# A new order of work, with the weights' casts on ScalarE and GpSimd, in attention followed by mixture of depths

## The chip, the cores and the metric

The kernel runs on one core of a Trainium2 chip. The core has TensorE (PE) for matrix products, VectorE (DVE), ScalarE (ACT) and GpSimd (POOL) for the rest, and SyncE (SP), which here only issues transfers. Each engine takes its instructions strictly in the order in which they were written, and waits for other engines or for transfers by semaphores. The metric is the time of one execution on the device in microseconds.

## The reference

The inputs are q, k and v of shape (8, 8, 576, 64): batch, heads, positions, head size. Attention is causal over a window of 128 positions, with a bias that falls with the distance at a slope of its own for each head. Its output, put together over the heads, is x of shape (8, 576, 512). Then each batch picks the 128 positions with the largest gate score and runs them through two matrices of weights:

```
scores = where(0 <= i - j < 128, q k^T / 8 - slope_h * (i - j), -1e9)
x      = softmax(scores) v                  (heads side by side: 512 columns)
s      = x . w_gate                         (one score a position)
top    = the 128 positions of largest s, for each batch
out    = x, and for positions in top:
out    = x + sigmoid(s) * (relu(x w1) w2)   (w1: 512x1024, w2: 1024x512)
```

All inputs and the output are 32-bit floats in main memory.

## The kernel before

The kernel works batch by batch. Within a batch, heads are taken in four pairs (c = 0 to 3), and the positions in five tiles of 128 (the last one half full). The steps of one batch b are small functions, and each has a one-letter name:

- Loads: `L` brings q or k, `l` brings v. All are issued by SyncE in the order before. Casts to bf16: `Q` for q and k (lines 315 to 323), `C` for v (lines 388 to 397). The cast helper `_cast` (line 304) uses ACT.copy on ScalarE, an affine_select with a condition that always holds on GpSimd (line 307), and tensor_copy on VectorE (line 313).
- `T`: transposes of q and k on TensorE (line 331) into one of two PSUM buffers named `mx`; `V`: the copy out of PSUM into qT or kT (lines 337 and 339), which frees that buffer.
- `S`: scores of one head pair, the bias and mask as products first (line 414), q times k after (line 430), into one PSUM buffer `sc`. `X`: one exponential of 128x2048 on ScalarE (line 439). `A`: product with v, which has a column of ones for the sum (lines 454 and 457), into one PSUM buffer `at`. `N`: division by the sum into x (lines 464 and 466, VectorE).
- `P`: the store of x to `out` (lines 477 and 481). `G`, `g` and `J`: gate scores (line 506, VectorE). `B`, `H`, `b`, `h`: the scores spread along a row. `M`: comparisons (line 547, VectorE), `R`, `r`: the rank of each position. `O`: a one-hot matrix of the picked positions (line 589 on GpSimd or 593 on VectorE). `K`, `k`: the list of picked positions.
- `D`: the picked rows of x as a product with the one-hot matrix (line 623), `v` the copy out; `W`, `w`: product with w1 (line 637) and relu (lines 647 and 649); `Z`, `z`: product with w2 (line 654), scaled by the gate (lines 661 and 664); `F`: GpSimd adds the result into the picked rows of `out` by an indirect transfer (line 667). Every `F` waits until the transfer of the `F` before it has landed.

The weights are loaded in eight chunks of 512 KB, `U0` to `U3` for w1 and `U4` to `U7` for w2 (lines 682 and 685), and cast by `d0` to `d7` (`cast_w`, line 690). A word d without an engine goes to VectorE at line 698. The chunks have no buffer of their own: they use two halves of `x_buf[2]`, one for even and one for odd chunks, so that a load waits for the cast of the chunk two before it. `x_buf[2]` then holds x of batches 4 and 7, so `N40` waits for the last weight cast.

Nothing decides the order at run time. The string ORDER (line 731) lists all 729 steps as words: the letter, the batch, the numbers of the step, and after a slash the engine (A, D, P, S) where there is a choice. The last lines of the kernel walk through it, so the order of the words is the order of each engine's queue, and the order in which buffers are handed on. `S13`, for example, is the scores of batch 1, pair 3; `C021/D` casts tile 2, half 1 of batch 0's v on VectorE; `V00t/D` copies the tail of batch 0's transposed q out of PSUM on VectorE.

The line that names the engine of a weight cast:

```
(load_w(int(name[1])) if f == "U" else cast_w(int(name[1]), e))
```

Of the kernel before, what the change touches and what calls it, by code (L numbers as in the profile page):

```python
# [26 lines left out]
def kernel(  # L27
# [376 lines left out]
    P, sc_t = {}, {}  # L404
# [274 lines left out]
    def load_w(i):  # L679
        t = wst[i] = w_flat[:, 1024 * (i % 2):1024 * (i % 2) + 1024]  # L680
        if i < 4:
            SP.dma_start(out=t, in_=moe_w1[128 * i:128 * (i + 1), :])
        else:
            i -= 4
            SP.dma_start(
                out=t.rearrange("p (c f) -> p c f", c=2),
                in_=moe_w2[256 * i:256 * (i + 1), :].rearrange(
                    "(c p) f -> p c f", p=128))
# [39 lines left out]
    def gate_spread(eng):  # L728
        _copy(eng, wg_bc.rearrange("p (i x) -> p i x", i=NDC), wg_t.pop("r"))

    ORDER = """
        c3 L011/S c0 L010/S L00t/S L001/S L000/S L01t/S l01 c1 L002/S
        qL l02 L003/S c2 L012/S l00 Q011/A L013/S L10 L11 l12 c6 T011
        Q010/D c8 Q00t/A c5 c7 T010 V011/A Q000/A Q01t/D V010/A T000
        c92 c4 Q001/A T00t V000/A C021/D T01t c90 V01t/A V00t/D Q002/A
        C031/D T001 S00 C041/D V001/A C020/P qT T002 X00 C030/P qe
        Q003/D Q012/D L20 l10 c91 C040/P T012 V002/A V012/D T003 S01
        C011/P C010/D qB X01 C000/D C001/D V003/D A00 Q013/D N00 T013
        L21 l11 S02 Q1000/P Q1011/A V013/D A01 Q1010/A Q1001/P qb/D
        X02 L30 N01 T102 T100 V102/D Q11t/P Q1111/A A02 c93 Q1110/P  # L740
        V100/A T112 N02 S03 C140/P V112/A T101 Q1100/P X03 V101/D
        Q1101/P T110 L31 V110/D T111 l22 Q2001/P l21 C141/A A03
        Q2011/P V111/A N03 l20 Q2010/P T202 Q2000/A S10 C111/P V202/D
        P00 P01 l32 C100/A C101/P T200 X10 T201 G02 G04 G00 Q21t/A S11
        G01 Q2100/A C110/A Q2110/P V200/D l30 V201/D T210 C120/P
        C121/A X11 C130/P L40 V210/D T212 C131/P A10 l31 G03 S12
        Q2111/P V212/D Q3011/A N10 Q3001/P H0 B0 X12 Q2101/P h0/D A11
        b0/D Q3010/P L41 T211 U1 M01 Q3000/P V211/A S13 M02 Q3110/P
        L50 U0 N11 X13 Q3100/P Q31t/P M03 A12 M00 C241/P T310 C231/A
        S20 N12 Q3101/P V310/A C221/P T301 M04 A13 C220/P V301/D  # L750
        C230/A R0 C201/P Q3111/A r0 T302 N13 C210/P T312 X20 C200/P
        V302/D P11 P10 C240/P G11 l42 E0 S21 V312/A L51 G10 C211/A X21
        G14 A20 T311 G13 T300 G12 V311/A S22 C340/P N20 O0/P V300/A H1
        A21 h1/D e0 X22 B1 N21 b1/D Q4000/A S23 M14 C301/P M12 E1 K0
# [16 lines left out]
        D2 X50 C510/P M34 k1 A43 C501/P M32 T610 v2/D C521/P C531/A
        S51 C511/P N43 V610/A W11 C530/P l70 X51 M30 C520/P T611 G42
        F0 l71 A50 G41 w11/A S52 P40 P41 G40 V611/A T601 G43 V601/A
        G44 B4 W20 N50 b4/A C640/P X52 Q7001/P H4 w20/D A51 Q7010/P
        h4/D T602 N51 R3 Q7000/P V602/A S53 Q7011/P r3 M40 C620/A T612
        C621/P A52 X53 V612/D T702 C600/P e3 Z1 O3/D C611/P N52 E4
        V702/A S60 C641/P z1/A M44 C631/P M41 A53 X60 Q7100/P M43 K2
        D3 k2 C610/P M42 C601/P N53 W21 v3/A C630/P Q71t/A W30 P50 G53
        F1 w21/A T700 G50 w30/A S61 G51 V700/A R4 G52 X61 T712 A60 r4
        Q7110/P V712/D T701 N60 Q7101/P B5 b5/A S62 G54 V701/A A61  # L780
        O4/D X62 H5 T710 Q7111/P h5/D e4 Z2 C740/P M54 N61 C720/P
        V710/A C710/P M52 S63 z2/A M53 C731/P M51 K3 A62 X63 C741/P k3
        T711 C721/P N62 D4 C730/P V711/A M50 C700/P A63 C711/P v4/A
        N63 S70 C701/P R5 X70 P60 G61 P51 P61 K4 r5 k4 W41 G60 E5 G63
        S71 w41/A G62 W31 X71 G64 A70 O5/P w31/D B6 N70 H6 S72 b6/A
# [107 lines left out]
```

The softmax here doesn't subtract the row's maximum and nothing guards it: scores larger than these inputs give would overflow.

## Time and profile before

| | before |
|---|---|
| time, median of 3 runs | 177.33 us (175.79 to 177.97) |
| span of the profiled execution | 175.2 us |
| TensorE busy | 130.3 us (74%) |
| VectorE busy | 133.5 us (76%) |
| ScalarE busy | 121.0 us (69%) |
| GpSimd busy | 105.1 us (60%) |
| moved by transfers | 44.38 MB, mean 253 GB/s |
| first exponential starts | 14.65 us |
| last exponential (X73) starts | 142.10 us |

A share of the span is an average over stages. The kernel has a start, in which the first loads, casts and transposes follow each other; a long middle, in which attention of one batch runs beside the transposes of the next and the second part of an earlier one; and a tail after the last exponential, in which only the picked positions are left. A line of a timeline gives the start, the duration, the engine, the line of the kernel, the operation with its tiles, and in brackets how long the engine had been idle before it and what ended that.

### The profile page before, as it was taken

Reading aid. Unit: us, or ns where it says so; the run is one execution under the profiler, and the core shown is the slowest. Engines: PE = TensorE matmul, PEld = TensorE weight load, DVE = VectorE, ACT = ScalarE, POOL = GpSimd, SP = SyncE. Lnnn points to the kernel's source line nnn. Section 1 sums busy time; section 2 is a strip of 40 time slices with the busy share of each in tenths; the row PEclk is TensorE's granted clock in tenths of the full one; section 3 lists DMA queues with packets and bytes.
Section 4 is the critical chain, followed back from the end, with each engine's and each line's share of the span. In section 5 each row is a group of like instructions: output and inputs, shape, how many; then the busy total and the mean of one; then the engine's idle time right before and its main releaser. Section 6 shows DMA issues by size and latency. Waiting matters only on the chain. (4 is left out here: it accounts for less than half of the span.)

```text
span 175.2 us, 5068 instructions
## 1 busy us (share of the span) xinstructions
PE 130.3 (74%) x2023; PEld 102.8 (59%) x2029; DVE 133.5 (76%) x383; ACT 121.0 (69%) x143; POOL 105.1 (60%) x171
## 2 busy tenths in 40 slices
PE   0426988667787866888974998999998999989100
PEld 0214766456665764576753787698697767686000
DVE  6655896999897899999955997999899997833000
ACT  4626497989979978449956899999887874532100
POOL 3761377599899917983318994988199903123330
PEclk9999999999969999699978999999999999999855
DMA  4899999999999995937999999999908044644224
GB/s 143 250 300 372 349 348 358 388 314 338 307 365 392 406 377 190 344 90 244 337 326 327 278 350 262 362 370 360 320 26 290 14 60 175 160 60 63 19 42 60
DMA packets 35216, 44.38 MB, mean 253 GB/s; under 512 B 1652, under 2 KB 24440, under 8 KB 35192
## 3 DMA queue, kind: packets, MB, share of 16 engines
q1 hardware_dynamic: 34040, 41.95, 73.5%
q0 software_dynamic: 1152, 2.10, 8.2%
q8 instruction: 16, 0.26, 0.6%
q14 instruction: 8, 0.07, 0.1%
HBM read 32.51 MB, written 11.53 MB: 251 GB/s over the span
## 5 line engine op out<-in xcount | busy, mean ns | idle before, releaser
L439 ACT ACTIVATE P<-sc 128x2048 bf16<-128x2048 f32 x32 | 60.1, 1879 | 16.0 <-PE sc L430 15.5
L307 POOL TENSOR_SCALAR_AFFINE_SELECT v_bf<-v_st 64x512 bf16<-64x512 f32 x47 | 34.0, 725 | 7.9 <-DMA v_st<-in_v_dram 5.5
L466 DVE TENSOR_TENSOR x<-at,rc 128x640 f32<-128x640 f32 x32 | 26.4, 824 | 4.7 <-POOL w_bf L307 3.6
L667 POOL DMA_INDIRECT out_dram<-fin,tok x8 | 13.0, 1629 | 23.2 <-ACT fin L661 9.0
L430 PEld LDWEIGHTS <-kT 64*128 64x128 bf16 x384 | 21.0, 115 | 9.7 <-issue 2.7
L506 DVE CUSTOM_DVE_ANT_0 x_bf<-x,wg_bc 128x512 bf16<-128x512 f32 x35 | 26.3, 799 | 0.2
L414 PE MATMUL sc<-mQ,mK 64*128 64x512 bf16 x128 | 21.6, 417 | 5.5 <-ACT P L439 5.1
L457 PE MATMUL at<-v_bf,P 128*128 128x66 bf16 x320 | 23.6, 196 | 2.2 <-DVE x L466 2.0
L331 PE MATMUL mx<-ident_bf,k_bf 128*128 128x128 bf16 x144 | 13.8, 235 | 13.3 <-DVE qT L339 5.7
L457 PEld LDWEIGHTS <-P 128*128 128x128 bf16 x320 | 21.0, 100 | 3.8 <-DVE x L466 2.0
L307 POOL TENSOR_SCALAR_AFFINE_SELECT k_bf<-k_st 128x512 bf16<-128x512 f32 (+1 forms) x32 | 19.8, 642 | 3.8 <-DMA k_st<-in_k_dram 3.2
L430 PE MATMUL sc<-qT,kT 64*128 64x256 bf16 (+2 forms) x384 | 22.0, 252 | 0.1
L454 PE MATMUL at<-v_bf,P 128*128 128x66 bf16 x256 | 21.5, 196 | 0.0
L547 DVE TENSOR_SCALAR_CACHE_REDUCE cmp<-row,sc_all 128x448 bf16<-128x448 f32 (+4 forms) x40 | 20.3, 537 | 0.3 <-ACT row L337 0.3
L331 PEld LDWEIGHTS <-k_bf 128*128 128x128 bf16 x144 | 10.0, 105 | 14.7 <-issue 7.7
L454 PEld LDWEIGHTS <-P 128*128 128x128 bf16 x256 | 18.4, 99 | 0.2
L637 PE MATMUL mx<-gx,w_bf 128*128 128x128 bf16 x256 | 16.3, 219 | 1.3 <-DVE rank L568 0.7
L331 PE MATMUL mx<-ident_bf,q_bf 128*128 128x128 bf16 x144 | 13.0, 230 | 4.8 <-ACT q_bf L311 2.2
L307 POOL TENSOR_SCALAR_AFFINE_SELECT v_bf<-v_tl 32x512 bf16<-32x512 f32 x13 | 9.0, 691 | 12.4 <-ACT kT L337 4.8
L337 ACT COPY kT<-mx 128x1024 bf16<-128x1024 bf16 (+1 forms) x19 | 13.9, 742 | 3.5 <-PE mx L331 3.4
L637 PEld LDWEIGHTS <-w_bf 128*128 128x128 bf16 x256 | 14.7, 98 | 2.1 <-issue 1.3
L654 PE MATMUL mx<-w_bf,hs 128*128 128x512 bf16 x58 | 14.6, 378 | 0.5 <-ACT kT L337 0.2
(104 smaller groups left out, 229.3 us busy)
## 6 DMA issues: line engine op xcount, KB each, us to landing
v_st<-in_v_dram SPq DMA_DIRECT2D x16, 512.0 KB, 8.7
out_dram<-x SPq DMA_DIRECT2D x8, 1024.0 KB, 8.4
q_st<-in_q_dram SPq DMA_DIRECT2D x7, 1152.0 KB, 9.5
k_st<-in_k_dram SPq DMA_DIRECT2D x14, 512.0 KB, 9.1
x<-in_moe_w_dram SPq DMA_DIRECT2D x8, 512.0 KB, 6.5
k_st<-in_k_dram SPq DMA_DIRECT2D x4, 256.0 KB, 4.3
q_st<-in_q_dram SPq DMA_DIRECT2D x4, 256.0 KB, 4.3
k_st<-in_k_dram SPq DMA_DIRECT2D x16, 64.0 KB, 8.3
```

The costliest lines, as they stand in the source:

```text
L307: POOL.affine_select(out=o, in_=i, compare_op=OP.is_ge, fill=0.0, base=1, pattern=[[0, n] for n in o.shape[1:]], channel_multiplier=0)
L331: PE.transpose(out=t[:, i, :], in_=qk_bf[b, w][:, r, :, :], identity=ident_bf)
L414: PE.matmul(out=sc[:, a, 512 * half:512 * half + 512], lhsT=mK[rows, c, :], rhs=(mQ[rows, :] if half else mQ[rows, None, 0:256].to_broadca ...
L430: PE.matmul(out=sc[:, a, c0:c0 + nq], lhsT=kc[rows, :], rhs=qt_[rows, S * c + q0:S * c + q0 + nq], start=False, stop=(c0 in (256, 832)))
L439: ACT.activation(out=p, in_=sc, func=AF.Exp, scale=scale)
L454: PE.matmul(out=o, lhsT=p[:, a, l:l + 128], rhs=vb[:, t - 1, h, :], start=True, stop=False)
L457: PE.matmul(out=o, lhsT=p[:, a, l:l + 128], rhs=vb[:, t, h, :], start=(t == 0), stop=True)
L466: DVE.tensor_tensor(out=xo[:, :, :, c, :], in0=av_[:, :, :, 0:D], in1=rc[:, :, :, None].to_broadcast([128, 2, NT, D]), op=OP.mult)
L506: DVE.tensor_tensor_reduce(out=part(x_bf[b][:, t, :]), in0=part(x32[b][:, t, :]), in1=part(wg_bc), scale=1.0, scalar=0.0, op0=OP.mult, op1 ...
L547: DVE.tensor_scalar(out=cmp_[b][:, t, 128 * t:], in0=row[b][:, 128 * t:], scalar1=sc_all[b][:, t:t + 1], scalar2=None, op0=OP.is_gt, op1=O ...
L637: PE.matmul(out=t[:, f, :], lhsT=w1_bf[:, dc, 128 * fg:128 * (fg + 1)], rhs=gx[b][:, dc, :], start=(dc == 0), stop=(dc == NDC - 1))
L654: PE.matmul(out=t, lhsT=hs[b][:, f, :], rhs=w2_bf[:, f, :], start=(f == 0), stop=(f == NFC - 1))
```

## The change

The order is replaced as a whole by one found in a new search. The search's model of the chip had all engines' durations lengthened by 4 per cent, and the transfers' rates as seen on the chip. The steps are the same 729; their order differs on every engine, and so does the engine of some of them. The w1 casts d0 to d3, which name no engine, now go to ScalarE in place of VectorE (line 695 in place of line 698); the w2 casts d4 to d7 stay on GpSimd. Five of the first loads are issued by ScalarE. It is meant to fit the order better to what the engines and transfers do on the chip.

The diff, cut to its start, to the words around the weights, to its end, and to the line in `do`:

```
     ORDER = """
-        c3 L011/S c0 L010/S L00t/S L001/S L000/S L01t/S l01 c1 L002/S
-        qL l02 L003/S c2 L012/S l00 Q011/A L013/S L10 L11 l12 c6 T011
-        Q010/D c8 Q00t/A c5 c7 T010 V011/A Q000/A Q01t/D V010/A T000
-        c92 c4 Q001/A T00t V000/A C021/D T01t c90 V01t/A V00t/D Q002/A
-        C031/D T001 S00 C041/D V001/A C020/P qT T002 X00 C030/P qe
...
-        Q2111/P V212/D Q3011/A N10 Q3001/P H0 B0 X12 Q2101/P h0/D A11
-        b0/D Q3010/P L41 T211 U1 M01 Q3000/P V211/A S13 M02 Q3110/P
-        L50 U0 N11 X13 Q3100/P Q31t/P M03 A12 M00 C241/P T310 C231/A
...
-        D0 Q4011/P X23 k0 M10 Q4001/P A22 M11 C320/P C331/A S30 v0/D
-        C341/P Q4010/A e1 C311/P N22 X30 T401 C330/P Q4100/P V401/D
-        A23 Q4110/P T400 M13 d1 T402 C321/P N23 S31 C300/P Q4111/A
-        V400/D Q41t/P X31 C310/P V402/D T410 A30 G21 T412 V410/A S32
-        G22 d0 R1 V412/D G20 X32 G23 U2 U3 l40 G24 B2 l41 N30 C440/P
...
-        Q5011/A T411 M21 Q5101/P V512/A V411/D d2 Q5100/P D1 Q5111/P
-        d3 S40 v1/D N32 X40 U5 W00 U4 L60 C400/P e2 C401/P W10 w00/D
...
-        C421/A M20 d5/P V511/A T502 N33 X41 W01 d4/P A40 G34 U6 U7 l52
-        L61 w01/A S42 l50 G30 V502/A G32 l51 X42 T501 G31 G33 P21 P20
-        L70 l62 l61 V501/D H3 d6/P Q6001/A h3/D l60 B3 E3 Q6010/A d7/P
-        R2 b3/D S43 C540/A P31 L71 r2 Q6000/P Q6011/A N40 T510 T600
...
-        h6/A e5 E6 A71 X72 M62 W40 M61 F2 N71 D5 w40/A M64 A72 v5/A
-        M60 S73 N72 K5 Z3 X73 k5 g73 g72 z3/A g74 A73 M63 Z4 F3 N73
-        g71 P70 P71 W50 z4/A g70 G73 W51 w50/A G71 G72 G74 R6 G70
-        w51/A J7 r6 H7 O6/D B7 h7/A Z5 b7/A e6 M72 M71 D6 z5/A M73 M70
-        F5 K6 v6/A k6 M74 E7 R7 e7 W61 F4 r7 O7/D w61/A K7 k7 D7 W60
-        v7/A W71 w60/A W70 w71/D Z6 w70/D Z7 z6/A F6 z7/A F7
+        L011/S c0 c3 L010/A L000/S L00t/A L01t/S c2 L001/A c6 L012/A
+        Q011/D c8 c5 L002/S c1 Q010/A c7 T011 qL Q000/D L10 Q00t/A
+        V011/A T000 l00 Q01t/D c4 l01 V000/A T010 l02 V010/A T00t
+        V00t/D L003/S Q001/D T01t V01t/A c90 T001 Q012/D Q002/A S00
+        c91 V001/D qT X00 qe T002 c93 T012 V012/D Q1001/P L013/A S01
...
+        Q21t/A L31 G00 Q2100/A T212 G04 A10 X11 G02 Q2110/P U1 G03
+        Q2000/A S12 U0 Q2010/A N10 C241/P T210 Q2001/P V212/A X12
...
+        C210/P X20 T310 L41 C230/P V311/D G10 d0 S21 G11 G13 X21 G12
+        V310/D Q3001/P B1 b1/A G14 T312 V312/A C231/P M02 H1 E1 d1 M00
+        Q4011/P A20 S22 M03 Q4010/P Q3011/A U3 M01 Q3000/P U2 h1/A M04
...
+        A22 C330/P C320/P M12 D0 P11 M10 Q4100/P L50 V401/A S30 P10
+        Q4110/P v0/D d3 C321/P N22 T410 Q4111/P T402 d2 e1 A23 Q4101/P
+        L51 V410/D X30 C340/P V402/D K0 C300/P N23 W01 U4 C341/A
...
+        W00 G24 l41 G23 A30 V411/A G20 S32 G22 w00/A T400 G21 X32 U5
+        R1 N30 Q5001/P Q5011/P V400/D A31 E2 Q5000/P Q5010/A S33 r1
+        N31 l40 Q5111/A Q5101/P T412 T502 X33 Q5110/P V412/D A32 d4/P
+        V502/D B2 O1/D H2 U6 C440/A S40 L60 Q51t/A C441/P b2/D h2/A
+        X40 C431/P N32 T511 T500 C430/P V511/D A33 d5/P C420/A S41 M24
+        M20 C421/A Q5100/P U7 D1 N33 V500/A C411/P l52 L61 C410/P
+        C401/A T510 e2 C400/P v1/A M22 V510/D d6/P X41 W11 M23 P21
+        T501 G33 A40 G31 l50 V501/A S42 G34 w11/A l51 d7/P M21 X42
+        T512 l62 V512/D R2 G32 Z0 r2 Q6011/P C541/A N40 C540/P Q6001/A
...
+        S72 N70 w40/A R5 X72 K3 G61 A71 r5 k3 H6 O5/P N71 B6 h6/A K4
+        b6/A S73 k4 E6 e5 A72 M62 X73 W41 M63 N72 D5 w41/A M61 K5 v5/A
+        A73 g72 k5 Z4 N73 g70 P71 Z3 z4/A G72 P70 G70 g73 F4 M60 z3/A
+        W50 G73 g74 F3 W51 w50/A g71 G74 R6 G71 w51/A M64 J7 r6 H7 B7
+        h7/D O6/D Z5 b7/A M72 M71 D6 z5/A M70 E7 F5 e6 v6/A M73 K6 k6
+        R7 M74 W60 r7 O7/D W61 w60/A e7 D7 w61/A Z6 v7/A W71 z6/A W70
+        F6 w71/D K7 w70/A k7 Z7 z7/A F7
     """
...
-            (load_w(int(name[1])) if f == "U" else cast_w(int(name[1]), e))
+            (load_w(int(name[1])) if f == "U" else cast_w(int(name[1]), e or ACT))
```

More of the change, by code (lines that the diff above doesn't have):

```diff
@@ L731 @@
     ORDER = """
-        c3 L011/S c0 L010/S L00t/S L001/S L000/S L01t/S l01 c1 L002/S
-        qL l02 L003/S c2 L012/S l00 Q011/A L013/S L10 L11 l12 c6 T011
-        Q010/D c8 Q00t/A c5 c7 T010 V011/A Q000/A Q01t/D V010/A T000
-        c92 c4 Q001/A T00t V000/A C021/D T01t c90 V01t/A V00t/D Q002/A
-        C031/D T001 S00 C041/D V001/A C020/P qT T002 X00 C030/P qe
-        Q003/D Q012/D L20 l10 c91 C040/P T012 V002/A V012/D T003 S01
-        C011/P C010/D qB X01 C000/D C001/D V003/D A00 Q013/D N00 T013
@@ L739 @@
[L739 to L746, printed above, removed]
@@ L747 @@
-        Q2111/P V212/D Q3011/A N10 Q3001/P H0 B0 X12 Q2101/P h0/D A11
-        b0/D Q3010/P L41 T211 U1 M01 Q3000/P V211/A S13 M02 Q3110/P
-        L50 U0 N11 X13 Q3100/P Q31t/P M03 A12 M00 C241/P T310 C231/A
[L750 to L754, printed above, removed]
@@ L755 @@
-        D0 Q4011/P X23 k0 M10 Q4001/P A22 M11 C320/P C331/A S30 v0/D
-        C341/P Q4010/A e1 C311/P N22 X30 T401 C330/P Q4100/P V401/D
-        A23 Q4110/P T400 M13 d1 T402 C321/P N23 S31 C300/P Q4111/A
-        V400/D Q41t/P X31 C310/P V402/D T410 A30 G21 T412 V410/A S32
-        G22 d0 R1 V412/D G20 X32 G23 U2 U3 l40 G24 B2 l41 N30 C440/P
-        Q5001/A S33 r1 Q5010/P Q5000/A H2 A31 O1/D b2/A E2 T500 N31
-        C441/P h2/A X33 Q4101/P V500/D A32 Q51t/P Q5110/P T512 M23
-        Q5011/A T411 M21 Q5101/P V512/A V411/D d2 Q5100/P D1 Q5111/P
@@ L763 @@
-        d3 S40 v1/D N32 X40 U5 W00 U4 L60 C400/P e2 C401/P W10 w00/D
-        C411/P C410/A M22 T511 C420/P M24 A33 C431/A w10/D C430/P S41
-        C421/A M20 d5/P V511/A T502 N33 X41 W01 d4/P A40 G34 U6 U7 l52
-        L61 w01/A S42 l50 G30 V502/A G32 l51 X42 T501 G31 G33 P21 P20
-        L70 l62 l61 V501/D H3 d6/P Q6001/A h3/D l60 B3 E3 Q6010/A d7/P
-        R2 b3/D S43 C540/A P31 L71 r2 Q6000/P Q6011/A N40 T510 T600
-        V510/A O2/D A41 Z0 X43 N41 C541/P Q6100/P l72 P30 M31 Q6111/P
-        A42 M33 V600/A Q6110/P z0/D S50 Q6101/P Q61t/A N42 K1 C500/P
@@ L771 @@
[L771 to L785, printed above, removed]
-        h6/A e5 E6 A71 X72 M62 W40 M61 F2 N71 D5 w40/A M64 A72 v5/A
@@ new lines @@
+        V00t/D L003/S Q001/D T01t V01t/A c90 T001 Q012/D Q002/A S00
+        c91 V001/D qT X00 qe T002 c93 T012 V012/D Q1001/P L013/A S01
+        c92 Q1000/P V002/A Q1010/A Q1011/P L11 X01 C001/P T101 T102
+        V101/D C000/P C010/P V102/D T100 C021/A C030/P S02 l12 C020/A
+        V100/D l11 C031/P C011/P Q003/A l10 C040/A C041/D T003 V003/D
+        Q013/A A00 T013 N00 X02 V013/D A01 Q1111/P L21 Q1100/A N01 S03
+        Q1110/P Q11t/A T112 Q1101/P X03 T110 V112/D C140/P T111 V110/D
+        L20 A02 C130/P V111/D l22 qB C121/P C120/A l21 N02 S10 C141/P
@@ new lines @@
+        C110/A l20 qb/D C100/P A03 X10 C111/P N03 C131/P C101/P S11
+        Q21t/A L31 G00 Q2100/A T212 G04 A10 X11 G02 Q2110/P U1 G03
+        Q2000/A S12 U0 Q2010/A N10 C241/P T210 Q2001/P V212/A X12
+        V210/D T200 Q2011/P A11 P01 V200/D Q2111/P T202 Q2101/P N11
+        C221/A S13 C220/P L30 V202/A T201 G01 X13 T211 C200/P V201/D
+        A12 C211/P V211/D B0 C201/P L40 E0 N12 H0 b0/A S20 Q3111/P P00
+        Q3100/A l31 C240/P h0/D A13 Q3101/A e0 Q3110/P N13 Q31t/A T311
+        C210/P X20 T310 L41 C230/P V311/D G10 d0 S21 G11 G13 X21 G12
@@ new lines @@
+        V310/D Q3001/P B1 b1/A G14 T312 V312/A C231/P M02 H1 E1 d1 M00
+        Q4011/P A20 S22 M03 Q4010/P Q3011/A U3 M01 Q3000/P U2 h1/A M04
+        R0 X22 N20 Q3010/P l32 T302 Q4000/P r0 A21 M14 O0/D V302/A
+        T301 l30 S23 Q4001/P N21 V301/A T300 C331/P X23 T401 V300/D
+        A22 C330/P C320/P M12 D0 P11 M10 Q4100/P L50 V401/A S30 P10
+        Q4110/P v0/D d3 C321/P N22 T410 Q4111/P T402 d2 e1 A23 Q4101/P
+        L51 V410/D X30 C340/P V402/D K0 C300/P N23 W01 U4 C341/A
+        C301/P l42 S31 k0 Q41t/A C310/P M13 w01/A M11 T411 C311/P X31
@@ new lines @@
+        T512 l62 V512/D R2 G32 Z0 r2 Q6011/P C541/A N40 C540/P Q6001/A
+        S43 G30 z0/A L70 A41 O2/D E3 l61 Q61t/A W10 Q6111/A P20 N41
+        Q6000/P l60 X43 H3 Q6101/P w10/D A42 Q6010/P h3/D T602 N42
+        C501/P D2 C510/A Q6110/P C511/A V602/D L71 A43 Q6100/P C521/A
+        S50 C531/P N43 v2/A C520/P C500/A K1 K2 k1 C530/P X50 k2 T612
+        e3 l70 B3 Q7000/P V612/D G44 T600 b3/A S51 G40 l71 V600/A G43
+        T611 X51 A50 C641/P V611/D T610 G42 W20 G41 P31 V610/A S52 N50
+        Q7010/P w20/A Z1 C640/P M30 X52 P30 Q7011/P M31 C620/P A51 M32
@@ new lines @@
+        C600/P T601 z1/A M33 S53 C611/P N51 V601/A Q7001/P P40 B4 E4
+        M34 l72 R3 X53 C630/P b4/D A52 P41 C610/P r3 H4 e4 W21 C621/P
+        h4/D N52 C631/A Q7100/P S60 w21/A C601/P M40 A53 X60 O3/P T701
+        M41 Z2 M44 N53 V701/A M43 S61 P51 Q7110/A M42 P50 z2/D A60
+        C711/P X61 D3 Q7101/P N60 Q7111/P R4 G50 F2 Q71t/A S62 v3/A
+        G52 A61 X62 G54 T711 r4 C730/P V711/D T700 C720/P N61 T710
+        V700/A C701/P S63 V710/A G53 F0 T712 G51 V712/A T702 X63 A62
+        V702/D C741/P B5 O4/P N62 H5 b5/A S70 h5/D E5 M51 C710/A A63
@@ new lines @@
+        M53 X70 W31 M54 N63 C731/P D4 M50 C740/P P61 C721/A S71 P60
+        C700/P M52 w31/A F1 G63 v4/A A70 X71 G60 W30 G62 W40 G64 w30/A
+        S72 N70 w40/A R5 X72 K3 G61 A71 r5 k3 H6 O5/P N71 B6 h6/A K4
[4 more added lines that the diff above has]
+        R7 M74 W60 r7 O7/D W61 w60/A e7 D7 w61/A Z6 v7/A W71 z6/A W70
```

## The prediction

> **What bounds the kernel now.** I first read the busy time by stage: the stretches run from the first exponential (L439, the 128x2048 ACTIVATE) of one batch to that of the next; the last stretch is everything after the last exponential. Columns: stretch, length, busy us and instructions of each engine, granted clock, DMA share, GB/s.
>
> ```profile
> 0.00:14.65 14.65, 4.79 (x37) 2.99 (x37) 8.13 (x42) 6.88 (x16) 7.79 (x44) 1.00 0.85 239
> ...
> 46.92:60.41 13.49, 10.74 (x170) 8.85 (x168) 11.62 (x36) 11.97 (x14) 12.55 (x18) 0.87 1.05 383
> 60.41:78.72 18.31, 13.79 (x219) 10.60 (x219) 18.10 (x35) 11.94 (x15) 12.48 (x19) 0.91 0.77 259
> 78.72:99.43 20.71, 15.90 (x247) 12.43 (x246) 16.29 (x42) 16.08 (x18) 10.20 (x13) 0.92 0.95 304
> ...
> 142.10:175.20 33.10, 19.34 (x233) 13.75 (x232) 12.29 (x52) 9.79 (x15) 7.74 (x5) 0.84 0.42 80
> ```
>
> Three places stand out. Batches 3 and 4 (60.41 to 99.43) take 39 us where batches 1 and 2 take 14.8 and 13.5: in batch 3 VectorE is busy 18.10 of 18.31 us, and DMA falls from 1.05 to 0.77. The start takes 14.65 us with no engine above 8.1. The tail takes 33.1 us with no engine above 19.3.
>
> The start next, in order of time on VectorE and then on TensorE:
>
> ```profile
> 10.53 0.42 DVE L313 CAST v_bf<-v_st 64x512 bf16<-64x512 f32 x1 [1.86 <-DMA v_st<-in_v_dram]
> 10.96 0.65 DVE L248 SCALAR_TENSOR_TENSOR mK<-tmp 128x128 bf16<-128x128 f32 x1
> 11.53 0.41 DVE L339 COPY qT<-mx 128x256 bf16<-128x256 bf16 x1
> ```
> ```profile
> 11.99 0.37 PE L331 MATMUL mx<-ident_bf,k_bf 128*128 128x128 bf16 x2 [3.24 <-DVE qT L339]
> ```
>
> The value cast C021/D stands in VectorE's queue ahead of the copy V00t/D. It waits 1.86 us for its load; behind it the copy holds one of two `mx` buffers, so TensorE idles 3.24 us before the last transposes that the first scores need.
>
> Then the waits of the load queue, and the moment at which the weights' chain meets VectorE:
>
> ```profile
> SPq L685 <- DVE w_bf L698: 6.1, 1, 6.1
> SPq L685 <- DMA x<-in_moe_w_dram: 6.1, 2, 3.2
> SPq L682 <- DVE w_bf L698: 5.6, 1, 5.6
> ```
> ```profile
> 91.50 1.04 POOL L307 TENSOR_SCALAR_AFFINE_SELECT w_bf<-x 128x1024 bf16<-128x1024 f32 x1 [6.61 <-DMA x<-in_moe_w_dram]
> ```
> ```profile
> 93.99 0.82 DVE L466 TENSOR_TENSOR x<-at,rc 128x640 f32<-128x640 f32 x1 [3.60 <-POOL w_bf L307]
> ```
>
> All eight weight chunks pass through two halves of `x_buf[2]`. A load U2 to U7 waits for the cast of the chunk two before it, and every load behind it in SyncE's queue waits too: 17.8 us in these three rows. Batch 4 writes its attention output to the same buffer, so N40 waits 3.60 us for the last cast.
>
> Last, the tail on GpSimd:
>
> ```profile
> 144.96 1.57 POOL L667 DMA_INDIRECT out_dram<-fin,tok  x1 [4.63 <-ACT fin L661]
> 152.82 1.54 POOL L667 DMA_INDIRECT out_dram<-fin,tok  x1 [6.29 <-DVE cmp L547]
> 157.64 1.54 POOL L667 DMA_INDIRECT out_dram<-fin,tok  x1 [3.28 <-DMA out_dram<-fin,tok]
> 163.53 1.54 POOL L667 DMA_INDIRECT out_dram<-fin,tok  x1 [4.35 <-ACT fin L661]
> 169.09 1.54 POOL L667 DMA_INDIRECT out_dram<-fin,tok  x1 [4.02 <-issue]
> ```
>
> Each scatter adds into `out` and waits until the one before it has landed; the last four are 4.82, 5.89 and 5.56 us apart, mean 5.4. The last one starts 5.7 us after its data are ready (fin done at 162.74 + 0.69), and the span ends 6.1 us after it starts.
>
> **What the Trainium skill says.** (1) "DMA: Bandwidth & Descriptors", Anatomy of one DMA: DMA engines never wait on semaphores, the issuing sequencer does. That is the SyncE blocking above, and the trace agrees (5.6 and 6.1 us). It also means that a load issued from ScalarE can hold up ScalarE. (2) The same page, Issuing engines are not separate DMA queues: a second issuing engine saves issue time only. Before has no load on ScalarE, so no run shows it yet; SyncE's issues at the start took about 0.5 us each. (3) "SBUF — State Buffer", Who interferes with whom: VectorE's copies, casts and tensor_scalar can contend with GpSimd, ScalarE never does. The trace agrees: a weight cast took 0.75 us at 62.31 with GpSimd idle and 1.20 us at 66.92 with it busy.
>
> **The change part by part.** Instruction counts come from the two orders, durations from the groups by shape before.
>
> Weight casts d0 to d3: VectorE loses 4 x 1.04 = 4.2 us. ScalarE has no such row; its 128x512 and 128x576 casts take 0.615 and 0.668, so 0.83 ns an element, which puts 1024 elements at 1.04. "ScalarE: Activation LUTs", Rules for kernel authors, prices 0.3 us + 0.83 ns per element, 1.15. I take 1.04 (+4.2 us; upper end 4.6). The w2 casts d4 to d7 were on GpSimd before and stay there.
>
> Transposed copies: eight 128x1024 kT copies go from ScalarE to VectorE, ScalarE -8 x 1.01 = -8.1, VectorE +8 x 0.68 = +5.4; two qT copies swap, about -0.25 on VectorE and +0.2 on ScalarE. MoE's PSUM copies go the other way: four hs, two gx and one row copy, VectorE -(2.7 + 1.4 + 0.7) = -4.8, ScalarE +(2.4 + 1.2 + 0.6) = +4.2. Five value casts leave VectorE (-2.2), three to ScalarE (+1.8) and two to GpSimd (+1.5); two value tails go from GpSimd (-1.4) to ScalarE (+1.2). Query and key casts: ScalarE -6 x 0.67 + 3 x 0.62 + 4 x 0.40 = -0.6; GpSimd +6 x 0.75 - 3 x 0.74 - 8 x 0.35 = -0.5. One one-hot goes from VectorE (-1.0) to GpSimd (5 x 0.85 = +4.2).
>
> Sums: VectorE -7.0 (133.5 to 126.5), ScalarE +2.9 (121.0 to 124), GpSimd +3.8 (105.1 to 109), TensorE nothing. No wait is removed by these sums alone; they count in stages where VectorE ends last.
>
> So I priced each order's words between the first exponentials of two batches with start-to-start spacings of the rows (scores 1.0 us, exponential 1.8, norm 0.98, gate 0.78, w1 half 0.9, w2 1.75 and so on) and took the fullest engine of each stage. Before: 13.3, 15.0, 12.5, 19.7, 15.8, 14.8, 16.1, 11.6, sum 118.8; the trace has 127.4 (14.65 to 142.1), so 8.7 us above the sum, of which batch 0 has 4.2 and batch 4 has 4.9. After: 13.6, 13.2, 16.0, 13.0, 17.5, 13.5, 15.9, 10.7, sum 113.4. VectorE's 19.7 of batch 3 is spread over its neighbours. Gain 5.4 us.
>
> Start: no value cast precedes V00t/D on VectorE any more, which can take up to 3.2 us of TensorE's idle time away. Against it, ScalarE issues k0, the query tail, q1 and k2 first (five issues x 0.5 = 2.5 us, the last one waiting for the first load, which landed at 3.57 before), and then loads its table (1.28 us). Its first cast Q010/A then starts near 6.5 where a first cast started at 3.57; from there the casts and copies Q010, Q00t, V011, V000, V010, V01t and Q002 take about 3.8 us in sum, TensorE's S00 1.9 us. First exponential at 12 to 13; I take 12.5, gain 2.1. L013/A, queued behind X00, also waits for a free DMA slot: up to 1 us, on the path of X01.
>
> Weights: U0 and U1 go out during batch 1, d0 to d3 run between X20 and X30 and d4 to d7 between X33 and X42, so U2 and U3 wait for ScalarE casts with batch 2 still running. New wait: d3 and d2 stand in ScalarE's queue ahead of X30, about 6.5 us after d1 lets U3 go; weight loads take 6.5 us (median) to land, 0 to 4 us of wait. Behind it stand X30 and so all of batch 3. d7 still precedes N40, with U7 behind the 1152 KB load L60: I keep 3 us there. I therefore leave the 8.7 us of excess as it was, the blocking of SyncE traded for these.
>
> Tail: it begins with F4 (z4 done 5.1 us after X73 starts, as before), and then F3, F5, F6, F7 chained behind it: 5.1 + 4 x 5.4 = 26.7, + 6.1 = 32.8 us, 30.5 to 34.8 with the shortest and longest spacing. TensorE has more left after X73, 21.3 us against 17.3 by the same prices; with waits z7 is done near 24.5, still before F7's turn. So Z6 ahead of W71 and W70, which frees F6 early, is hidden by the chain. I take 33.0, no gain.
>
> Sum: 12.5 + 113.4 + 8.7 + 33.0 = 167.6 us of span. The timed median is 2.1 above the profile's span before, so 169.7; I say 169.5.
>
> **Rivals.** (a) The gain goes into waits for loads: DMA share is already over 1 in batches 0 to 2, and one weight cast on ScalarE waits as long as GpSimd's longest did (6.6 us). 175.2 - 2.1 - 5.4 + 6.6 + 2.1 = 176.4, no change. For it: 335 to 383 GB/s in the full stages. Against: the DMA idle time around 72 to 79 us is room. (b) Slower: all of GpSimd's 10.2 us of waits for weights move to ScalarE, ahead of exponentials, and the tail grows by TensorE's 4 us: 175.2 - 2.1 - 5.4 + 10.2 + 4 + 2.1 = 184. For it: ScalarE's queue is strictly in order. Against: counted in bytes, 12.8 MB go ahead of and with U0 and U1, 19 MB with U2 and U3; at the 360 GB/s of batches 0 to 2, two us after the start, they land near 38 and 55 us, and d0 and d3 come up near 44 and 58. (c) Better: excess falls to 3 us, the chain keeps its shortest spacing: 12 + 113.4 + 3 + 31 + 2.1 = 161.5.
>
> **Chances.** Forecast case, 165 to 173.8: 0.62; (c) 0.10; (a) 0.17; (b) 0.11. Faster 0.72, same 0.17, slower 0.11. The range leaves out (b) and the lower half of (c), and reaches over (a) to 177.5; its low end is 163.5.
>
> **What would show it.** First exponential at 12 to 13 us; no VectorE wait on v_st before it; VectorE busy near 126; batches 3 and 4 together 33 to 35 us instead of 39; SyncE's waits for w_bf below 8 us in sum; X73 near 134; the last five scatters about 5.4 us apart with F7 waiting for F6. It is wrong if ScalarE waits over 5 us for weights, if X73 starts after 138, or if TensorE rather than the scatters ends the tail. A lower granted clock (0.94 on average before) would blur all of it.

## The result and the profile after

The changed kernel takes 184.80 us (median of 4 runs, 184.65 to 185.47); the kernel before, on the same chip, 176.56 us (median of 4, 173.49 to 177.97). The ratio is 1.0589, with a 95% interval of 1.0462 to 1.0716: slower, where 169.5 us was predicted. Ratios leave out disturbed executions, in which a kernel runs some per cent longer; where a kernel had too few others, its median over all executions stands alone, and the trace shown of a run can be one of a disturbed execution.

The page of the changed kernel, busy time of each engine:

```profile
PE 137.0 (75%) x2029; PEld 107.0 (58%) x2029; DVE 127.1 (69%) x374; ACT 123.0 (67%) x152; POOL 106.2 (58%) x171
```

VectorE fell from 133.5 to 127.1 us as worked out, and no engine is busier than 137 us of a span of 183.1. The time is in waits. Busy time by stage of the changed kernel, columns as in the prediction's first table:

```profile
0.00:12.57 12.57, 4.90 (x37) 3.07 (x37) 7.34 (x43) 5.26 (x13) 6.08 (x41) 1.00 0.85 279
12.57:31.41 18.84, 13.58 (x181) 10.47 (x182) 11.84 (x26) 13.39 (x16) 13.53 (x21) 1.00 0.93 267
31.41:45.27 13.86, 10.52 (x197) 8.71 (x195) 11.18 (x26) 13.10 (x16) 7.79 (x12) 1.00 1.03 320
45.27:65.34 20.07, 16.23 (x210) 12.34 (x209) 14.84 (x40) 15.30 (x17) 13.54 (x21) 0.74 1.06 384
65.34:81.69 16.35, 13.31 (x219) 10.87 (x217) 14.53 (x34) 12.53 (x17) 11.57 (x14) 0.90 1.08 354
81.69:99.31 17.62, 16.23 (x291) 13.48 (x291) 16.86 (x41) 17.28 (x22) 13.79 (x18) 1.00 1.04 324
...
128.29:146.77 18.48, 13.11 (x199) 10.51 (x195) 9.50 (x34) 9.32 (x11) 10.16 (x16) 0.82 0.40 95
146.77:183.10 36.33, 22.07 (x290) 16.48 (x287) 14.34 (x61) 11.23 (x17) 8.15 (x6) 0.88 0.39 69
```

Batches 3 and 4 (65.34 to 99.31) take 34.0 us instead of 39.0: the sum that the prediction gave for the two came out. At the start of batch 7 (X70 at 128.29, before at 130.81) the changed kernel is still 2.5 us ahead. Batch 7, from 128.29 to 146.77, is the odd row: 18.48 us, no engine above 13.2, against 11.29 us before. The tail adds 3.2 us to the 33.1 of before.

What happens in batch 7 stands in GpSimd's timeline of the changed kernel:

```profile
117.99 1.75 POOL L667 DMA_INDIRECT out_dram<-fin,tok  x1 [0.79 <-DVE fin L664]
124.19 2.58 POOL L307 TENSOR_SCALAR_AFFINE_SELECT v_bf<-v_st 64x512 bf16<-64x512 f32 x3 [4.45 <-DMA out_dram<-fin,tok]
126.93 1.58 POOL L667 DMA_INDIRECT out_dram<-fin,tok  x1 [0.16 <-POOL v_bf L307]
131.94 0.65 POOL L307 TENSOR_SCALAR_AFFINE_SELECT v_bf<-v_tl 32x512 bf16<-32x512 f32 x1 [3.43 <-DMA out_dram<-fin,tok]
132.69 2.94 POOL L589 TENSOR_SCALAR oh<-krow,rank 128x128 bf16<-128x128 f32 x5
```

The two L667 rows are the scatters F2 and F0. Directly behind each stands a cast of v (C730 and C741), and each cast starts only when the scatter has landed (at 123.66 and 131.72): 4.45 and 3.43 us of idle GpSimd. The wait belongs to the program: each scatter raises a semaphore of its own when it lands, and in the trace waits of line 307 for just these two semaphores stand in front of the two casts. Behind the second cast stands the one-hot O4. TensorE's timeline shows who needs it:

```profile
133.36 0.22 PE L623 MATMUL mx<-oh,x_bf 128*128 128x128 bf16 x1 [3.75 <-POOL oh L589]
...
135.68 1.87 PE L623 MATMUL mx<-oh,x_bf 128*128 128x128 bf16 x16 [0.31 <-POOL oh L589]
137.48 1.04 PE L414 MATMUL sc<-mQ,mK 64*128 64x512 bf16 x4
```

TensorE takes D4 (L623) ahead of S71 (L414), so the scores of pair 1 wait for the one-hot, and X71 starts at 139.47, 11.18 us after X70. ScalarE and VectorE stop with it:

```profile
137.59 0.59 ACT L337 CAST gx<-mx 128x512 bf16<-128x512 f32 x1 [6.16 <-PE mx L623]
```
```profile
137.59 0.73 DVE L506 CUSTOM_DVE_ANT_0 x_bf<-x,wg_bc 128x512 bf16<-128x512 f32 x1 [6.51 <-PE mx L623]
```

The kernel before has the same wait once with idle time, behind F1, in batch 6. In its GpSimd timeline

```profile
118.34 1.71 POOL L667 DMA_INDIRECT out_dram<-fin,tok  x1 [0.28 <-POOL v_bf L307]
120.11 2.07 POOL L307 TENSOR_SCALAR_AFFINE_SELECT k_bf<-k_st 128x512 bf16<-128x512 f32 x3
126.51 0.65 POOL L307 TENSOR_SCALAR_AFFINE_SELECT v_bf<-v_tl 32x512 bf16<-32x512 f32 x1 [4.34 <-DMA out_dram<-fin,tok]
```

the casts of k behind the scatter run at once, and the cast of v after them waits 4.34 us. It is over before X70, and X70 to X73 took 11.29 us there; what the wait costs in batch 6 (15.93 us) was not tried. Which casts take over the scatter's wait was readable in the trace of before, and I did not read it.

ScalarE's timeline of the changed kernel shows the second loss, in batch 0:

```profile
12.57 1.88 ACT L439 ACTIVATE P<-sc 128x2048 bf16<-128x2048 f32 x1 [1.51 <-PE sc L430]
17.67 0.38 ACTq L118 DMA_DIRECT2D k_st<-in_k_dram  x1
18.08 0.59 ACT L337 COPY qT<-mx 128x512 bf16<-128x512 bf16 x1 [3.64 <-DMA v_st<-in_v_dram]
```

X00 is over at 14.45. The issue of the k load L013/A goes out only at 17.67, when an earlier load has landed: for 3.2 us the issue holds ScalarE. Behind it stand a copy of qT and X01.

Last, the scatters of the tail in the changed kernel (F4, F3, F5, F6, F7):

```profile
152.90 1.59 POOL L667 DMA_INDIRECT out_dram<-fin,tok  x1 [5.74 <-ACT fin L661]
159.49 1.54 POOL L667 DMA_INDIRECT out_dram<-fin,tok  x1 [5.00 <-ACT gexp L574]
165.05 1.54 POOL L667 DMA_INDIRECT out_dram<-fin,tok  x1 [4.02 <-ACT gx L337]
171.70 1.54 POOL L667 DMA_INDIRECT out_dram<-fin,tok  x1 [5.10 <-ACT fin L661]
177.09 1.54 POOL L667 DMA_INDIRECT out_dram<-fin,tok  x1 [3.85 <-issue]
```

They are 6.59, 5.56, 6.65 and 5.39 us apart, mean 6.05, in place of 5.4. The names in the brackets mislead: ScalarE finished F6's data (z6) at 166.32, long before 171.70, so what F6 waited for is the landing of F5. The last z7 is done at 170.80, 6.3 us before F7 starts, so TensorE does not end the tail.

### The profile page after: what moved, and what is told of

The parts are those of the page before. It is cut to its first block, busy times and chain, and to the rows that moved or that the text cites. A ratio compares the mean times of both kernels' runs of the same rounds, so it can differ in the third digit from the quotient of the medians.

```text
span 183.1 us, 5080 instructions
## 1 busy us (share of the span) xinstructions
PE 137.0 (75%) x2029; PEld 107.0 (58%) x2029; DVE 127.1 (69%) x374; ACT 123.0 (67%) x152; POOL 106.2 (58%) x171
## 5 line engine op out<-in xcount | busy, mean ns | idle before, releaser
L506 DVE CUSTOM_DVE_ANT_0 x_bf<-x,wg_bc 128x512 bf16<-128x512 f32 x35 | 28.0, 843 | 6.5 <-PE mx L623 6.5
L457 PE MATMUL at<-v_bf,P 128*128 128x66 bf16 x320 | 24.5, 199 | 5.3 <-DVE x L466 4.3
L667 POOL DMA_INDIRECT out_dram<-fin,tok x8 | 12.9, 1616 | 24.8 <-ACT fin L661 10.8
L414 PE MATMUL sc<-mQ,mK 64*128 64x512 bf16 x128 | 22.4, 432 | 4.9 <-ACT P L439 4.7
L457 PEld LDWEIGHTS <-P 128*128 128x128 bf16 x320 | 21.5, 101 | 5.6 <-DVE x L466 5.0
L307 POOL TENSOR_SCALAR_AFFINE_SELECT q_bf<-q_st 128x576 bf16<-128x576 f32 x22 | 17.2, 803 | 11.0 <-DMA q_st<-in_q_dram 10.7
L430 PE MATMUL sc<-qT,kT 64*128 64x256 bf16 (+2 forms) x384 | 22.8, 258 | 0.0
L454 PE MATMUL at<-v_bf,P 128*128 128x66 bf16 x256 | 22.3, 199 | 0.0
L547 DVE TENSOR_SCALAR_CACHE_REDUCE cmp<-row,sc_all 128x320 bf16<-128x320 f32 (+4 forms) x40 | 20.1, 537 | 0.2
L454 PEld LDWEIGHTS <-P 128*128 128x128 bf16 x256 | 18.9, 101 | 1.4 <-issue 1.2
L339 DVE COPY qT<-mx 128x768 bf16<-128x768 bf16 (+2 forms) x14 | 12.2, 878 | 10.8 <-PE mx L331 10.6
L331 PE MATMUL mx<-ident_bf,q_bf 128*128 128x128 bf16 x144 | 15.4, 259 | 4.9 <-issue 3.0
L307 POOL TENSOR_SCALAR_AFFINE_SELECT k_bf<-k_st 128x512 bf16<-128x512 f32 x21 | 14.4, 701 | 4.6 <-DMA k_st<-in_k_dram 3.4
L623 PE MATMUL mx<-oh,x_bf 128*128 128x128 bf16 x160 | 11.8, 229 | 5.1 <-POOL oh L589 5.1
```

The source lines that it names most:

```text
L307: POOL.affine_select(out=o, in_=i, compare_op=OP.is_ge, fill=0.0, base=1, pattern=[[0, n] for n in o.shape[1:]], channel_multiplier=0)
L331: PE.transpose(out=t[:, i, :], in_=qk_bf[b, w][:, r, :, :], identity=ident_bf)
L414: PE.matmul(out=sc[:, a, 512 * half:512 * half + 512], lhsT=mK[rows, c, :], rhs=(mQ[rows, :] if half else mQ[rows, None, 0:256].to_broadca ...
L430: PE.matmul(out=sc[:, a, c0:c0 + nq], lhsT=kc[rows, :], rhs=qt_[rows, S * c + q0:S * c + q0 + nq], start=False, stop=(c0 in (256, 832)))
L454: PE.matmul(out=o, lhsT=p[:, a, l:l + 128], rhs=vb[:, t - 1, h, :], start=True, stop=False)
L457: PE.matmul(out=o, lhsT=p[:, a, l:l + 128], rhs=vb[:, t, h, :], start=(t == 0), stop=True)
```

## The experiments

All edits but the casts' engine are to the string ORDER; the diffs show the words around what moves. Times are medians, beside the kernel before in the same set of runs.

**The scatters F2 and F0 late, just ahead of F1.**

```
-R4 G50 F2 Q71t/A S62
+R4 G50 Q71t/A S62
...
-G53 F0 T712
+G53 T712
...
-w31/A F1 G63
+w31/A F2 F0 F1 G63
```

> The order after, with the scatters F2 and F0 moved behind the last casts, just ahead of F1. Theory A (GpSimd's queue: each of the two scatters holds the cast behind it until it has landed, 4.45 and 3.43 us, so the one-hot O4 comes late, and with it D4 and S71): the step from exponential X70 to X71 falls from 11.2 us to about 4 us and the time by 5 to 8 us, to 177 to 180. Rival B (the pause comes from something else, the ranking of batch 4 or a lower clock): X70 to X71 stays over 9 us, time within 1.5 us of 184.8. Rival C (the weights' casts on ScalarE are what costs): no change either.

Measured: 179.69 us, ratio 1.0249 (1.0087 to 1.0411). X70 to X71 falls from 11.18 to 3.65 us, though the mean granted clock of this trace is the lower one (0.907, 0.921). The stop in batch 7 therefore comes from what stands behind the two scatters. But the gain is partly lost again: GpSimd's timeline of this kernel

```profile
132.08 1.76 POOL L667 DMA_INDIRECT out_dram<-fin,tok  x1 [0.18 <-issue]
137.30 1.69 POOL L667 DMA_INDIRECT out_dram<-fin,tok  x1 [3.46 <-DMA out_dram<-fin,tok]
143.53 1.56 POOL L667 DMA_INDIRECT out_dram<-fin,tok  x1 [4.54 <-DVE rc L464]
144.55 3.48 POOL L589 TENSOR_SCALAR oh<-krow,rank 128x128 bf16<-128x128 f32 x5
154.85 1.61 POOL L667 DMA_INDIRECT out_dram<-fin,tok  x1 [6.82 <-ACT fin L661]
```

has all eight scatters after 132 us, and five of them after 154.

**The k load of tile 3 issued by SyncE.**

```
-T012 V012/D Q1001/P L013/A S01 c92
+T012 V012/D Q1001/P L013/S S01 c92
```

> The order after, with the load L013 issued by SyncE in place of ScalarE. Theory A2 (ScalarE stands 3.2 us behind X00, waiting for a free DMA slot): X01 starts near 16 in place of 19.1 us, the first batch ends 2 to 3 us earlier; the end moves by 1 to 3 us, less what the later wait at O4 takes back. Rival (loads bound the first batch anyway): X01 earlier, but X10 within 1 us of 31.4 and the time within 1 us.

Measured: 182.00 us, ratio 1.0452 (1.0357 to 1.0546). X01 starts at 16.30 instead of 19.14 and X10 at 27.44 instead of 31.41, so the issue does stand on the path of batch 0. X70 comes at 122.86, 5.4 us earlier, but X70 to X71 then takes 12.5 us: the stop behind F0 takes part of the gain back.

**Where the casts run, alone: the kernel before with d0 to d3 on ScalarE, and the changed order with them on VectorE.**

```
-cast_w(int(name[1]), e))
+cast_w(int(name[1]), e or ACT))
...
-cast_w(int(name[1]), e or ACT))
+cast_w(int(name[1]), e or DVE))
```

> The order before, with the casts d0 to d3 on ScalarE: the named part of the change alone. Theory A: worth little by itself, minus 2 to plus 2 us (VectorE gets 4.2 us back in batches 3 and 4, ScalarE gives them). Rival C: slower by 4 us or more, since exponentials stand behind casts that wait for loads.

Measured: 179.10 us (175.67 to 180.01) beside 175.54 for the kernel before. In its profile batch 3 shrinks from 18.3 to 17.3 us and batch 4 grows from 20.7 to 23.5. No ratio; nothing speaks for a gain, and rival C's loss of 4 us or more is not excluded.

> The order after, with the casts d0 to d3 back on VectorE: the new order alone. Theory A: still slow, 182 to 188, X70 to X71 still 10 to 12 us. Rival C: the loss goes, 176 to 179.

Measured: 183.04 us, ratio 1.0494 (1.0358 to 1.0629), X70 to X71 still 11.3 us. The casts' engine is not what made the change slow; the order, with the engines that its words name, is.

**The store P00 early**, since in batch 2 of the changed kernel a norm waits 2.78 us for it.

```
-A11 P01 V200/D
+A11 P01 P00 V200/D
...
-Q3111/P P00 Q3100/A
+Q3111/P Q3100/A
```

> The order after, with the store P00 moved ahead of the loads L30 and L40, right behind P01. Theory A3 (N20 waits 2.8 us for batch 0's store, which stands behind 2.3 MB of loads): N20 no longer waits for the store, batch 2 takes 17 to 18 us in place of 20.1, the time falls by 1 to 3 us. Rival (batch 2 is long because TensorE's clock was 0.74 there, or because the loads that now come later are waited for in turn): batch 2 stays over 19 us, or batch 3 gives the gain back; time within 1 us of 184.8.

Measured: 184.15 us, ratio 1.0342 (1.0208 to 1.0477). The wait is gone, batch 2 still takes 18.8 us (20.07), and X70 to X71 takes 12.6. Most of batch 2's length is something else, and the time is within 1 us of the changed kernel's, as the rival had it.

**The scatter F3 ahead of F4.** Its product Z3 and copy z3 move with it.

```
-r5 k3 H6 O5/P N71
+r5 k3 Z3 H6 z3/A O5/P F3 N71
...
-P71 Z3 z4/A G72
+P71 z4/A G72
...
-F4 M60 z3/A W50 G73 g74 F3
+F4 M60 W50 G73 g74
```

> The order after, with Z3 and z3 moved ahead (behind k3) and the scatter F3 ahead of F4, so that four scatters in place of five are left behind z4. Theory A4 (the chain of scatters sets the end): F7 starts at X73 plus 24 to 26 us in place of 30.3, the time falls by 4 to 6 us. Rival (TensorE's products set the end): F7 waits for z7, not for F6, and the time falls by 2 us or less.

Measured: 179.21 us, ratio 1.0149 (1.0066 to 1.0232): 5.6 us below the changed kernel by their medians, taken in different sets of runs. F3 goes at 147.91, just before X73 (149.49), and F7 starts 24.7 us after X73 instead of 30.3. One scatter fewer behind X73 shortens the tail by about one spacing. It has a price ahead of X73, where Z3 and z3 now stand: X72 to X73 takes 5.5 us instead of 3.4, here and in every run below with this move. In these two traces X71 starts at the same time (139.46, 139.47), and F7 2.9 us earlier.

**Together**: L013/S, F2 and F0 ahead of F1 and P00 early, as above, and the one-hots O4 and O5 on VectorE.

```
-C741/P B5 O4/P N62
+C741/P B5 O4/D N62
...
-k3 H6 O5/P N71
+k3 H6 O5/D N71
```

> The order after with L013 on SyncE, F2 and F0 behind the last casts, O4 and O5 on VectorE, and P00 early. Theory A: X70 to X71 under 4 us, X73 at 131 to 136; the tail then has eight scatters of 5.6 us from about 126 on, F7 at 165 to 168, time 172 to 176. Rival (the order as a whole is worse, its moves give back elsewhere): X73 after 139, time over 178.

Measured: 179.19 us, ratio 1.0134 (1.0039 to 1.0229). X70 to X71 is 3.65 us, but X73 comes at 141.34, past the 139 that the rival named, and F7 at 172.93.

**The same with the early F3, and F0 far ahead, before batch 6's first q cast.**

```
-N41 Q6000/P
+N41 F0 Q6000/P
...
-F2 F0 F1
+F2 F1
```

> As e7_combo, with Z3 and F3 early and F0 ahead of the cast Q6000, where its data have long been ready. Theory A with A4: six scatters from about 128 on or the last products set the end; X73 at 132 to 137, time 165 to 171, below the kernel before. Rival: the early F0 holds GpSimd's casts of batch 6 for 5 us and X73 comes after 140, time over 175.

Measured: 174.99 us, ratio 0.9884 (0.9764 to 1.0004). F0's wait moved with it, as the rival had it: GpSimd's casts stop for 3.72 us, until F0 has landed, and go on at 99.63, and X51 to X52 takes 9.4 us. Casts of q and k and one of v ran behind F0 at once; the wait stands in front of a later cast of v. Batch 5 takes 20.27 us.

**F0 directly behind F2.**

```
-N41 F0 Q6000/P
+N41 Q6000/P
...
-F2 F1
+F2 F0 F1
```

> The combined order with the early output scatter F3, but with scatter F0 put directly behind F2, just ahead of F1, and no longer ahead of batch 6's first q load on GpSimd. Theory (a scatter in GpSimd's queue holds up the casts and relu work queued behind it): batch 5 falls from 20.3 us to 14.5-16.5, X70 comes near 124-126, X70 to X71 stays under 4.5 us, last scatter at X73 + 24 to 27, time 168-172 us, ratio 0.95-0.98 to the kernel before. Rival (two scatters back to back before F1 push the tail's chain later by as much as batch 5 gains): last scatter at X73 + 29 or more, time 174-177.

Measured: 172.43 us beside 176.68, ratio 0.9778 (0.9657 to 0.9900). Batch 5 takes 15.05 us, X70 comes at 126.76 and X71 3.65 us later, F7 at X73 + 24.6. In GpSimd's timeline four scatters follow each other with no computing between them, so their waits hold up no cast:

```profile
121.52 1.76 POOL L667 DMA_INDIRECT out_dram<-fin,tok  x1 [0.18 <-DVE kT L339]
126.57 1.57 POOL L667 DMA_INDIRECT out_dram<-fin,tok  x1 [3.29 <-DMA out_dram<-fin,tok]
132.06 1.94 POOL L667 DMA_INDIRECT out_dram<-fin,tok  x1 [3.92 <-DMA out_dram<-fin,tok]
138.15 1.55 POOL L667 DMA_INDIRECT out_dram<-fin,tok  x1 [4.15 <-ACT row L337]
```

**The q load of batch 3 earlier**, to ask what makes batch 2 long.

```
-Q21t/A L31 G00
+Q21t/A L30 L31 G00
...
-C220/P L30 V202/A
+C220/P V202/A
```

> As e9_f0_late, with the q load of batch 3 (L30) moved ahead of L31, so that it is issued much earlier. Theory L (batch 2's 20 us come from GpSimd waiting for that load): the wait of 3.5 to 5.6 us on q_st there goes to under 1 us and batch 2 takes 16.5-18 us, time 2 us or more below e9_f0_late. Theory C (batch 2 is slow because TensorE's granted clock falls to about 0.74 there): batch 2 stays at 19-20.5 us with the wait gone, time within 1 us of e9_f0_late.

Measured: 171.69 us, ratio 0.9726 (0.9631 to 0.9820), the lowest median here, but too near to the run before it to be called faster. Neither theory is right as put. GpSimd's waits for q fall from 7.1 us to 3.5, not under 1, and batch 2 from 20.3 to 18.1 us; but batch 1 and batch 3 grow, and the three together take 50.8 us instead of 51.4. The clock alone does not do it either: with d0 to d3 on VectorE (below) batch 2 took 19.56 us at a granted clock of 0.74, here with the casts on ScalarE it took 20.32 at 0.83 before the load was moved. What sets batch 2 at 18 to 20 us stays open.

**The changed kernel with O4 alone on VectorE.**

```
-C741/P B5 O4/P N62
+C741/P B5 O4/D N62
```

> The changed kernel with one edit: the one-hot of token tile 4 (O4) on VectorE, where it stood in the kernel before, and not on GpSimd behind the scatters F2 and F0. Theory (TensorE's dispatch product D4 waits for the one-hot, that waits for GpSimd's queue behind the scatters, and S71 stands behind D4): X70 to X71 falls from 11.2 us to 4-6.5, X73 comes 4-7 us earlier, time 178-181 us. Rival (the casts of k and v that stand behind the same scatters hold batch 7 as long): X70 to X71 stays at 9 us or more and the time at 183-185 us.

Measured: 180.76 us, ratio 1.0235 (1.0136 to 1.0335). X70 to X71 falls to 3.65 us, but X71 to X72 becomes 10.31, so the rival is half right. GpSimd and TensorE in this kernel:

```profile
132.07 0.65 POOL L307 TENSOR_SCALAR_AFFINE_SELECT v_bf<-v_tl 32x512 bf16<-32x512 f32 x1 [3.32 <-DMA out_dram<-fin,tok]
```
```profile
134.90 0.22 PE L457 MATMUL at<-v_bf,P 128*128 128x66 bf16 x1 [5.06 <-POOL v_bf L307]
```

With the one-hot out of the way, the product A70 waits for the very casts of v behind F0. Batch 7 as a whole gains only 1.2 us (17.33 for 18.48); 2.0 us of the rest were already there at X70. What has to move is the scatter, not one of those waiting behind it.

**The late-F0 order with d0 to d3 on VectorE**, by the second edit of the casts' engine above.

> As e9_f0_late, with the four first weight casts (d0 to d3) on VectorE and not on ScalarE. If moving these casts to ScalarE is worth something where nothing else blocks: VectorE is busy 3 to 4 us longer, ScalarE 4.6 us less, and the time is 1-3 us above e9_f0_late. If not (neither engine sets batches 3 and 4): within 1 us of e9_f0_late.

Measured: 172.40 us, ratio 0.9774 (0.9659 to 0.9888), against 172.43 with them on ScalarE. VectorE is busy 134.0 instead of 131.0 us, ScalarE 119.5 instead of 123.4, and the time is the same: in this order the named part of the change is worth nothing measurable.

**The changed kernel with its scatters alone placed anew**: F2 and F0 ahead of F1, F3 early, by the edits of the first experiment and of the early F3; all else as the change has it.

> The changed kernel with only its scatters placed anew: F2 and F0 just ahead of F1, and Z3, its copy z3 and F3 early, F3 behind the one-hot O5 and ahead of F4. The k load of tile 3 stays on ScalarE, the one-hots on GpSimd, P00 where the change put it. Theory (the places of the scatters alone make the change slower than before): X70 to X71 under 4.5 us, last scatter at X73 + 24 to 27, time 173-177 us, ratio 0.98-1.00 to the kernel before. Rival (the ScalarE load of tile 3 is a cause of its own of 3 us or more): 178-181 us, ratio 1.01-1.03.

Measured: 175.33 us (172.59 to 177.17) beside 175.57 for the kernel before (171.44 to 180.00). By these medians over all executions the changed kernel was 8.2 us above the kernel before (184.80, 176.56) and this one is 0.2 below. By the two lowest times of each, the changed kernel was 10.1 us above, and this one is 1.8 above (172.59 and 174.32 beside 171.44 and 171.84). So the places of the scatters account for most of the loss, without an interval; whether what may be left is noise or the load L013/A, this run does not tell. X70 to X71 is 3.65 us. The last scatter was expected 24 to 27 us after X73 and comes 30.7 after, because O4 still runs on GpSimd ahead of F2 (3.80 us in this trace), which goes only at 126.73; from there the eight scatters follow each other to 169.18 without a gap, 6.06 us each.

**The late-F0 order with the k load back on ScalarE.**

```
-Q1001/P L013/S S01
+Q1001/P L013/A S01
```

> The best order so far (F0 behind F2, early F3, one-hots on VectorE) with the k load of tile 3 back on ScalarE, as the change has it. If the 3.2 us in which that load's issue held ScalarE lie on the path: X10 at 30.5 to 31.5 us against 27.6, end 2.5 to 4.5 us later, time 175-177 us. If later stages take it up (batch 2 runs at a low TensorE clock and waits for loads in any case): X10 late all the same, but time within 1 us of 172.4.

Measured: 174.03 us (171.30 to 175.18). X10 is late, 30.42 against 27.55; X40 is 1.7 us late, X70 1.2 and F7 1.3. The held ScalarE costs 2.9 us where it happens, and in these two traces about 1.3 us of it reach the end: both answers of the expectation are half right.

## Why the prediction was wrong

- **Start: right.** First exponential at 12.57 (12.5), and no VectorE wait for v before it.
- **Weights: right, and beside the point.** The casts on ScalarE took 1.15 us each, as the Trainium skill's "ScalarE: Activation LUTs", Rules for kernel authors, prices them, where I took 1.04 from the smaller casts. ScalarE waited 0.42 us for a chunk, SyncE 2.8 us for casts of chunks, and N40 not at all. VectorE's sum (126.5 predicted, 127.1) and that of batches 3 and 4 (33 to 35, 34.0) came out, the second in part by luck: I had kept 3 us for N40 in batch 4, and batch 3 took 3.4 us more than its entry in the table. My reading of SyncE's three rows before was too wide, too: the middle one, 6.1 of the 17.8 us, is a wait for an earlier weight load and not for a cast.
- **The table of fullest engines: the step that failed.** It gave the batches 113.4 us plus 8.7 us of kept excess, 122.1 in all; they took 134.2, 12.1 us more, and X73, forecast near 134, came at 146.77. Over the table the batches took 20.8 us more, by batch 5.2, 0.7, 4.1, 3.4, 0.1, 1.5, -1.9 and 7.8. For batch 7 the table had its fullest engine, 10.7 us, and nothing for GpSimd standing idle behind F2 and F0. It booked the one-hot, "One one-hot goes from VectorE (-1.0) to GpSimd (5 x 0.85 = +4.2)", as busy time on an engine that is not full, and not as work that comes after a scatter's landing and ahead of S71. I named what stands behind the waiting instruction for d3 and for L013/A, and not for F2 and F0. The runs with the scatters moved late (X70 to X71 at 3.65 us in place of 11.18), with O4 moved (the stop goes over to the casts of v) and with the scatters alone moved show that this is the cause of the stop in batch 7. What batches 2 and 3 took beyond the table, 4.1 and 3.4 us, stays open.
- **L013/A: mis-sized.** "Up to 1 us" was 3.2 us of held ScalarE, and batch 0 took 5.2 us more than its table entry; with the load on SyncE the batch took 15.00 us for 18.84. I had the mechanism, also from the skill's "DMA: Bandwidth & Descriptors", Anatomy of one DMA, and here the trace agrees with it on ScalarE. Less than half of it reached the end (1.3 of 2.9 us, in the traces of the last experiment).
- **Tail: the form right, the size not.** 33.0 became 36.33 = 6.13 (F4 after X73, 5.1 predicted) + 4 x 6.05 (5.4) + 6.0. F4's transfer here has a 1 MB store of x issued at 151.7 ahead of it, which may explain the first 6.59 us; that was not tried. "Hidden by the chain" was right of Z6: the chain was the bound. The five scatters behind X73 I had counted; what I mis-sized is the first start and each spacing. That one of the five could go earlier, for a tail 5.6 us shorter and an X73 about 2 us later, I did not ask.
- **The rivals.** (b) had nearly the right time, 184, and the wrong reason: the weights' waits that it put on ScalarE were 0.42 us, and the tail grew by 3.2 us through the scatters and not through TensorE.

The same "DMA: Bandwidth & Descriptors", Rules for kernel authors, says that an accumulating transfer beside another access of the same bytes can lose a write, so that the earlier one's completion has to be waited for. That holds between the store of a batch and the scatter of the same batch. Two scatters of different batches add into different rows of `out`, so the page does not ask for the chain between them; the kernel has it all the same, in every order here, and no run left it out. With the chain kept, an order has two costs to weigh: a scatter with casts of v behind it can stop GpSimd, and a scatter put off lengthens the tail.

## What to carry to other kernels

Before summing busy time, list the few instructions on each queue that wait for a transfer, and read what stands behind each and who needs that; an engine that is 58% busy stopped the others for 7.5 us here (X70 to X71, 11.18 us and 3.65 with the scatters moved). A serial chain of transfers is a resource like an engine: ask first whether it has to be one, then count its links and take their spacing; place links before the last compute stage, weigh that against what their products delay there, and put nothing urgent between two of them. Moving work off a full engine need not be worth anything: in the order where it was tried with the scatters out of the way, the weights' casts made no measurable difference between ScalarE and VectorE.

## What the runs showed of the hardware

- GpSimd stood idle for 3.3 to 4.5 us before some casts of v that came after a scatter, until the scatter had landed; casts of k directly behind the scatter F1 of before started at once. The difference is in the program: in each of the 16 traces GpSimd has exactly one wait for the landing of each scatter but the last, either at the next scatter or at a cast of v before it. Why the program has it at casts of v and at none of q or k is not shown.
- A scatter of 256 KB took 1.5 to 2.0 us of issue on GpSimd and landed 4.5 to 9.5 us after its start, half of them within 4.9; one that had only the landing before it to wait for started 4.8 to 8.7 us after that one.
- A load issued from ScalarE after the start held it for 3.2 us in one kernel and 2.4 us in another before the issue went out.
